# Attention and gated MLP on one core: features dealt to partitions in runs of five instead of chunks of 128

## The chip, the cores and the metric

The kernel runs on one core of one Trainium2 chip. The metric is the device time of one execution in microseconds (us); the time of a kernel is the median of several runs.

## What is computed

One block over 2048 tokens of 640 features (bf16): a LayerNorm without gain or bias, then windowed attention (32 heads of 20, window of 8 positions that are 2 apart) and a bilinear gated MLP (1536 wide) side by side. The reference, cut to what matters:

```python
xn = (x - mean(x)) / sqrt(var(x) + 1e-5)
q, k, v = split(xn @ wqkv)                      # 640 -> 3 x 640
logits[s, w] = q[s] . k[s - 2 * w] / sqrt(20)   # w = 0..7, masked before the start
o = (softmax(logits) * v[s - 2 * w]).sum(w) @ wo
h = (xn @ w_gate) * (xn @ w_up)                 # 640 -> 1536
out = x + o + h @ w_down
```

## The kernel before, in words

A token's features must lie on partitions to be contracted by TensorE (PE): a matmul sums over the 128 partitions of its two operands, and the 640 features make five such sums (NCH = 5 "chunks"), accumulated in PSUM. Every weight with the features as rows is therefore held as [128 partitions, 5 chunks, columns]: `WQKV` (three groups of 640 columns), `WG` and `WU` (1536 columns). The normalised activations are held in `XNT` as [128 partitions, 5 chunks, 2048 tokens]. For a sum over features it doesn't matter which feature lies on which partition and chunk, as long as the weights and XNT agree. Before, feature 128c + p lies on partition p of chunk c.

The tokens come in 16 tiles of 128. A tile of x is loaded with tokens on partitions into `XST` (14 slots), so its 640 features are one row. VectorE (DVE) takes the statistics in two halves (`ln_stats_a`, `ln_stats_b`, lines 372 and 378), merges them (`ln_aggr`, line 384); ScalarE takes the square root (line 385), DVE the reciprocal (`ln_rstd`, line 404). `ln_apply` (line 419) writes (x - mean) * rstd into `XNS`, a ring of four slots, with a tensor_scalar instruction. Tile 1 has its sums from ScalarE (`ln_sums`). Then the tile is turned:

- tiles 0 to 3 (NTP = 4) by PE, chunk by chunk (`ln_pe`, line 434), into PSUM, and from there into XNT by DVE or ScalarE (`ln_copy`, lines 445 and 447). For tile 0, `ln_apply` writes chunk 0 first and the other four after it; for tile 1, two chunks and then three.
- tiles 4 to 15 by a DMA transpose that the SP queue issues (line 423), straight from XNS into XNT. SP issues its DMAs in program order: behind the transpose of tile 7 stand the loads of x for tiles 13 to 15, behind that of tile 15 `late_loads`, the mask, WG and WU.

The first stage of PE is laid out by hand (lines 713 to 780). It warms up, transposes tile 0, projects queries for it (`proj_tile`, line 492) and tile 1, then keys of both tiles in a loop over chunks (line 773), in the middle of which, ahead of chunk 2's second and chunk 3's first matmul, the transposes of tiles 2 and 3 stand. After that come queries and keys of tiles 2 and 3 (`proj_wide`, line 499), and then blocks of 512 tokens (`proj`, line 475): values of the first block (25 matmuls), queries and keys of the second (tiles 4 to 7), the third and the fourth, then the other values. `ln_pace` puts LayerNorm's steps for the later tiles between these in program order, by a modelled time of 1.45 us a tile; since each engine has its own queue, that fixes only the order on ScalarE and DVE.

The weights of queries and keys come as ten loads of one chunk each (`wqkv_load`, SP queue), those of values as one. The weight columns are read by PE with a step of five (`wcols`), so that output feature 5i + m of a projection lands on partition i of group m; this step is along the columns and is in both versions.

Behind LayerNorm DVE multiplies queries with shifted keys (line 522), adds, and sums over a head's partitions by DMAs (lines 533 and 545); softmax follows (lines 551 to 582, the exponential on ScalarE), then the products with values (line 605). PE meanwhile runs the MLP: gate and up (`glu`, line 638), evacuated by ScalarE (line 640) and multiplied by DVE (line 643), and the down projection together with `wo` (lines 665 and 697). The order of all this comes from a list of work for PE (`fill`) that is dealt out between DVE's steps by modelled durations (`step`, `run_fill`, lines 852 to 874). PSUM's eight banks go round in a ring.

Of the kernel before, what the change touches and what calls it, by code (L numbers as in the profile page):

```python
# [11 lines left out]
NCH = 5  # L12
# [199 lines left out]
def build_kernel(nc, A_x, A_wqkv, A_wo, B_x, B_w_gate, B_w_up, B_w_down, out):  # L212
# [80 lines left out]
    def dma(o, i, r=(), w=(), name="", eng="sp", group=None):  # L293
        return op(eng, lambda e: e.dma_start(o, i), r=r, w=w, dma=True, name=name, group=group)  # L294
# [15 lines left out]
    def x_load(t, eng="sp"):  # L310
        dma(XST[:, t % NXS, :], xhbm[t * TS:(t + 1) * TS, :], w=[XST[:, t % NXS, :]], name=f"xld{t}", eng=eng)

    def x_load2(t):
        dst = XST[:, t % NXS:t % NXS + 2, :]
        dma(dst, xhbm[t * TS:(t + 2) * TS, :].rearrange("(u p) n -> p u n", p=TS), w=[dst], name=f"xld{t}")

    wqkv_src = A_wqkv.rearrange("(c p) n -> p c n", p=128)

    def wqkv_load(g, c=None, eng="sp"):
        cs = slice(0, NCH) if c is None else c  # L320
# [23 lines left out]
    def late_loads():  # L344
        dma(MASK[0:128:4], MSK0[0:32], r=[MSK0[0:32]], w=[MASK[0:128:4]], name="mask")
        for T, src in ((WG, B_w_gate), (WU, B_w_up)):
            dma(T[:], src.rearrange("(c p) n -> p c n", p=128), w=[T[:]], name="ld_w")

    def down_loads():
        dma(WD[:], B_w_down.rearrange("(c p) n -> p c n", p=128), w=[WD[:]], name="ld_wd")  # L350
# [49 lines left out]
    def ln_rstd(t):  # L400
        if t >= NT:
            return
        sd, rstd = SD[:, t, 0:1], SD[:, t, 1:2]
        op("dve", lambda e: e.reciprocal(rstd, sd), r=[("sd", t)], w=[("rstd", t)], name=f"rstd{t}")

    def ln_apply(t, between=None):
        if t >= NT:
            return
        x, xs, mv = XST[:, t % NXS, :], XNS[:, t % NXN, :], MV[:, t, 0:2]
        sd, rstd = SD[:, t, 0:1], SD[:, t, 1:2]  # L410
        op0 = ALU.add if t == 1 else ALU.subtract
        mean = ("nm", t) if t == 1 else mv
        if between is None:
            ln_rstd(t)
        else:
            between()
        for c0, c1 in {0: ((0, 128), (128, D)), 1: ((0, 256), (256, D))}.get(t, ((0, D),)):
            o, i = xs[:, c0:c1], x[:, c0:c1]
            op("dve", (lambda o, i: lambda e: e.tensor_scalar(o, i, mv[:, 0:1], rstd, op0=op0, op1=ALU.mult))(o, i),
               r=[i, mean, ("rstd", t)], w=[o], name=f"lnap{t}")  # L420
        if t >= NTP:
            o = XNT[:, :, t * TS:(t + 1) * TS]
            op("sp", lambda e: e.dma_start_transpose(o, xs), r=[xs], w=[o], dma=True, name=f"xT{t}")
        if t == 7:
            x_load(13)
            x_load2(14)
        if t == NT - 1:
            late_loads()
# [35 lines left out]
    def wcols(which, c, m):  # L464
        return WQKV[:, which, c, m:D:NCH]
# [252 lines left out]
    ln_sums(1, 1)  # L718
    ln_sums(1, 2)
    ln_apply(0)  # L720
    ln_pe(0)
    ln_copy(0, (0, 1, 2))
    ln_apply(1)
    warm(2, TS)

    def ln_next(t):
        ln_stats_b(t)
        ln_aggr(t)
        ln_stats_a(t + 1)
        ln_apply(t)  # L730
# [35 lines left out]
    for c in range(NCH):  # L766
        for m in range(NCH):
            if (c, m) in ((2, 1), (3, 0)):
                tr(c)
            o = PS[:, bm, 2 * TS:] if m == 4 else PS[:, 3 + m // 2, m % 2 * 2 * TS:(m % 2 + 1) * 2 * TS]  # L770
            l, x = wcols(1, c, m), XNT[:, c, 0:2 * TS]
# [182 lines left out]
def bass_parallel_sum__sliding_local_dilated__glu_gated_bilinear__prompt_kernel(  # L954
    nc, A_x, A_wqkv, A_wo, B_x, B_w_gate, B_w_up, B_w_down, out
):
    build_kernel(nc, A_x, A_wqkv, A_wo, B_x, B_w_gate, B_w_up, B_w_down, out)
# [28 lines left out]
```

## Time and profile before

| what | us |
|---|---|
| median of 7 runs | 252.62 |
| lowest and highest | 252.32, 253.22 |
| the profiled execution | 252.96 |
| its span, first to last instruction | 251.7 |
| PE busy | 247.4 |
| DVE busy | 215.9 |
| ScalarE (ACT) busy | 114.7 |
| GpSimd (POOL) busy | 32.6 |

PE, PEld, DVE, ACT and POOL are the engines, PEld being PE's weight loads; SPq is the SP queue. A line of groups gives the line of the code, the engine, the operation, what it writes and reads with its shape, how often it ran, then the busy time in us, the mean of one in ns, and the idle time of the engine just before it with what ended it. A line of the timeline gives the start in us, the duration in us, engine, line and operation; in brackets stands how long the engine was idle before and what it waited for. Where several instructions are merged (x2), the duration runs from the start of the first to the end of the last.

### The profile page before, as it was taken

Reading aid. Unit: us, or ns where it says so; the run is one execution under the profiler, and the core shown is the slowest. Engines: PE = TensorE matmul, PEld = TensorE weight load, DVE = VectorE, ACT = ScalarE, POOL = GpSimd, SP = SyncE. Lnnn points to the kernel's source line nnn. Section 1 sums busy time; section 2 is a strip of 40 time slices with the busy share of each in tenths; the row PEclk is TensorE's granted clock in tenths of the full one; section 3 lists DMA queues with packets and bytes.
Section 4 is the critical chain, followed back from the end, with each engine's and each line's share of the span. In section 5 each row is a group of like instructions: output and inputs, shape, how many; then the busy total and the mean of one; then the engine's idle time right before and its main releaser. Section 6 shows DMA issues by size and latency. Waiting matters only on the chain.

```text
span 251.7 us, 3246 instructions
## 1 busy us (share of the span) xinstructions
PE 247.4 (98%) x1274; PEld 129.0 (51%) x1294; DVE 215.9 (86%) x255; ACT 114.7 (46%) x203; POOL 32.6 (13%) x41
## 2 busy tenths in 40 slices
PE   8999999999999999999999999999999999999997
PEld 3895555555544444444444444444444444445775
DVE  4799699999999962999999994799999999997212
ACT  5486667555555557555555551315555111011000
POOL 1000001043345222002231101002000000200200
DMA  6999869854787473255369972197600011490561
GB/s 186 298 284 168 126 141 411 223 111 79 146 146 135 72 137 54 113 224 97 70 121 254 393 230 42 33 334 61 96 0 3 21 26 36 59 131 21 79 154 52
DMA packets 33775, 33.78 MB, mean 134 GB/s; under 512 B 17984, under 2 KB 30272, under 8 KB 33728
## 3 DMA queue, kind: packets, MB, share of 16 engines
q1 hardware_dynamic: 27280, 24.13, 34.4%
q0 software_dynamic: 6192, 9.31, 22.9%
q8 instruction: 10, 0.16, 0.3%
q10 hardware_dynamic: 288, 0.13, 0.2%
q14 instruction: 5, 0.04, 0.1%
HBM read 14.42 MB, written 4.59 MB: 76 GB/s over the span
## 4 chain that ended last, share of the span: by engine, by line
PE 95%; DMA 2%; SPq 2%; issue 1%; DVE 0%
PE PS L638 41%; PE PS L665 22%; PE PS L475 21%; PE PS L697 7%; PE PS L499 2%; DMA WQKV<-in_A_wqkv_dram 2%; SPq L294 2%; PE PS L773 1%; PE PS L434 0%; DVE FOUT L701 0%
## 5 line engine op out<-in xcount | busy, mean ns | idle before, releaser
L638 PE MATMUL PS<-XNT,WU 128*128 128x512 bf16 x237 | 59.0, 379 | 0.2
L638 PE MATMUL PS<-XNT,WG 128*128 128x512 bf16 x232 | 57.9, 379 | 0.4
L475 PE MATMUL PS<-XNT,WQKV 128*128 128x512 bf16 x245 | 53.7, 379 | 0.3
L605 DVE TENSOR_TENSOR PVB<-VO,ATB 128x10240 f16<-128x10240 bf16 x8 | 43.9, 5489 | 0.2
L475 PEld LDWEIGHTS PS<-XNT,WQKV 128*128 128x128 bf16 x250 | 29.4, 118 | 24.4
L640 ACT ACTIVATE USX<-PS 128x512 bf16<-128x512 f32 x48 | 28.7, 597 | 22.6 <-PE PS L638 22.6
L638 PEld LDWEIGHTS PS<-XNT,WU 128*128 128x128 bf16 x240 | 23.5, 98 | 28.3
L638 PEld LDWEIGHTS PS<-XNT,WG 128*128 128x128 bf16 x240 | 23.5, 98 | 28.3
L600 DVE TENSOR_TENSOR PVB<-PVB 128x5120 f16<-128x5120 f16 (+1 forms) x16 | 34.5, 2154 | 0.3
L533 POOL DMA_DIRECT2D LOG<-PE x24 | 21.6, 912 | 60.6 <-DMA LOG<-PE 60.6
L640 ACT ACTIVATE HT<-PS 128x512 bf16<-128x512 f32 x36 | 21.5, 597 | 16.4 <-PE PS L638 16.4
L671 ACT ACTIVATE DT<-PS 128x512 f16<-128x512 f32 x15 | 8.9, 596 | 42.3 <-PE PS L665 39.2
L665 PE MATMUL PS<-HT,WD 128*128 128x512 bf16 x118 | 27.4, 379 | 0.1
L522 DVE TENSOR_TENSOR TMP<-QH,KH 128x2048 f16<-128x2048 bf16 x16 | 19.1, 1216 | 0.0
L665 PEld LDWEIGHTS PS<-HT,WD 128*128 128x128 bf16 x120 | 11.7, 98 | 14.2
L522 DVE TENSOR_TENSOR PP<-QH,KH 128x2048 f16<-128x2048 bf16 x16 | 18.9, 1217 | 0.0
L527 DVE TENSOR_TENSOR PP<-PP,TMP 128x4096 f16<-128x4096 f16 x8 | 18.3, 2291 | 0.2
L665 PE MATMUL PS<-VO,WO 128*128 128x512 bf16 x74 | 18.4, 379 | 0.0
L701 DVE TENSOR_TENSOR FOUT<-PS,XR 128x320 bf16<-128x320 f32 (+2 forms) x9 | 4.1, 454 | 15.0 <-PE PS L697 15.0
L533 POOL DMA_DIRECT2D PE<-PP x8 | 8.4, 1045 | 61.6 <-DVE PP L528 61.6
L482 ACT ACTIVATE VO<-PS 128x512 bf16<-128x512 f32 x20 | 11.9, 597 | 8.9 <-PE PS L475 8.8
L643 DVE TENSOR_TENSOR HT<-HT,USX 128x512 bf16<-128x512 bf16 x36 | 14.3, 415 | 1.7 <-ACT USX L640 1.7
(71 smaller groups left out, 221.4 us busy)
## 6 DMA issues: line engine op xcount, KB each, us to landing
PE<-PP POOLq DMA_DIRECT2D x8, 512.0 KB, 5.0
ATB<-LOG SPq DMA_DIRECT2D x8, 512.0 KB, 4.8
LOG<-PE POOLq DMA_DIRECT2D x24, 128.0 KB, 2.7
WG<-in_B_w_gate_dram SPq DMA_DIRECT2D x1, 1920.0 KB, 8.1
WU<-in_B_w_up_dram SPq DMA_DIRECT2D x1, 1920.0 KB, 14.7
WD<-in_B_w_down_dram SPq DMA_DIRECT2D x1, 1920.0 KB, 11.6
out_dram<-in_A_x_dram SPq DMA_DIRECT2D x1, 1920.0 KB, 10.6
out_dram<-FACC POOLq DMA_DIRECT2D x3, 640.0 KB, 6.7
```

Source lines behind the costliest of these rows:

```text
L475: op("pe", (lambda l, x, c: lambda e: e.matmul(PS[:, b, :], l, x, start=(c == 0), stop=(c == NCH - 1)))(l, x, c), r=[l, x], w=[PS[:, b, :] ...
L482: op("act", lambda e: e.activation(o, PS[:, b, :], ACT.Copy, scale=sc), r=[PS[:, b, :]], w=[o], name=f"pev{which}_{m}_{j}")
L522: return (1.22, lambda: op("dve", lambda e: e.tensor_tensor(o, qw, kw, ALU.mult), r=[q, k], w=[o], name=f"prod{h}_{p}_{c}"))
L527: (2.3, lambda: op("dve", lambda e: e.tensor_tensor(a, a, b, ALU.add), r=[a, b], w=[a], name=f"psum{h}_{p}")),
L533: op("pool", lambda e: e.dma_start(o, i, accum_op=ALU.add), r=[o, i], w=[o], dma=True, name=name)
L600: return lambda: op("dve", lambda e: e.tensor_tensor(o, x, y, ALU.add), r=[x, y], w=[o], name=f"{name}_{b}")
L605: lambda: op("dve", lambda e: e.tensor_tensor(PVB[:], vw, aw, ALU.mult), r=[v, a], w=[PVB[:]], name=f"pv_{b}")),
L638: op("pe", (lambda l, x, c: lambda e: e.matmul(PS[:, b, :], l, x, start=(c == 0), stop=(c == NCH - 1)))(l, x, c), r=[l, x], w=[PS[:, b, :] ...
L640: op("act", lambda e: e.activation(o, PS[:, b, :], ACT.Copy), r=[PS[:, b, :]], w=[o], name=f"guev{which}_{m}_{j}")
L643: h_pending.append(lambda: op("dve", lambda e: e.tensor_tensor(h, h, o, ALU.mult), r=[h, o], w=[h], name=f"h{m}_{j}"))
L665: op("pe", (lambda l, x, i: lambda e: e.matmul(PS[:, b, :], l, x, start=(i == 0), stop=(i == n - 1)))(l, x, i), r=[l, x], w=[PS[:, b, :]], ...
L697: op("pe", (lambda l, x, i, b, wid: lambda e: e.matmul(PS[:, b, 0:wid], l, x, start=(i == 0), stop=(i == n - 1)))(l, x, i, b, wid), r=[l, ...
```

## The change

Feature 5p + c now lies on partition p of chunk c, for the weights that are contracted over the features of the normalised activations: `WQKV`, `WG` and `WU`. The weights' rows are taken as "(p c)" instead of "(c p)". LayerNorm's write puts the features into the row of XNS in the new order (chunk by chunk, and within a chunk features c, 5 + c, 10 + c and so on), so its source is read with a step of five elements; the destination is the same row as before. Everything behind XNS is as it was: the transposes, XNT's shape, the matmuls and their number, and what comes out of them but for the order of summation. `WD` and `WO` are not touched.

```diff
-    wqkv_src = A_wqkv.rearrange("(c p) n -> p c n", p=128)
+    wqkv_src = A_wqkv.rearrange("(p c) n -> p c n", p=128)
...
         for T, src in ((WG, B_w_gate), (WU, B_w_up)):
-            dma(T[:], src.rearrange("(c p) n -> p c n", p=128), w=[T[:]], name="ld_w")
+            dma(T[:], src.rearrange("(p c) n -> p c n", p=128), w=[T[:]], name="ld_w")
...
         for c0, c1 in {0: ((0, 128), (128, D)), 1: ((0, 256), (256, D))}.get(t, ((0, D),)):
-            o, i = xs[:, c0:c1], x[:, c0:c1]
+            o = xs[:, c0:c1].rearrange("q (c p) -> q c p", p=128)
+            i = x.rearrange("q (p c) -> q c p", c=NCH)[:, c0 // 128:c1 // 128]
             op("dve", (lambda o, i: lambda e: e.tensor_scalar(o, i, mv[:, 0:1], rstd, op0=op0, op1=ALU.mult))(o, i),
                r=[i, mean, ("rstd", t)], w=[o], name=f"lnap{t}")
```

## The prediction, as put on record before the change was run

> **What bounds the kernel now.** I read the page's busy times first, then the chain that ended last, then the timeline of the first 40 us (the only stretch whose instructions the change touches), and last the idle times of VectorE (DVE) further on.
>
> ```profile
> PE 247.4 (98%) x1274; PEld 129.0 (51%) x1294; DVE 215.9 (86%) x255; ACT 114.7 (46%) x203; POOL 32.6 (13%) x41
> PE 95%; DMA 2%; SPq 2%; issue 1%; DVE 0%
> ```
>
> TensorE (PE) is busy from end to end and makes up 95% of the chain. Behind the start there is no gap in it: whatever delays PE in the first 25 us comes out at the end in full, and whatever delays only DVE costs nothing until PE waits for it. Now the start, from the timeline:
>
> ```profile
> 9.95 0.40 DVE L419 TENSOR_SCALAR XNS<-XST,MV,SD 128x640 bf16<-128x640 bf16 x1
> 10.60 0.45 DVE L419 TENSOR_SCALAR XNS<-XST,MV,SD 128x640 bf16<-128x640 bf16 x1
> 10.84 0.30 PE L773 MATMUL PS<-XNT,WQKV 128*128 128x256 bf16 x1 [0.28 <-DMA WQKV<-in_A_wqkv_dram]
> 11.69 0.44 PE L434 MATMUL PS<-IDENT,XNS 128*128 128x128 bf16 x5
> 12.11 0.49 DVE L372 BATCH_NORM_STATS2 STATS<-XST 128x6 f32<-128x320 bf16 x1 [0.40 <-DMA XST<-in_A_x_dram]
> 14.57 6.30 SPq L423 DMA_TRANSPOSE XNT<-XNS  x4
> 18.44 0.39 DVE L419 TENSOR_SCALAR XNS<-XST,MV,SD 128x640 bf16<-128x640 bf16 x1
> 18.74 21.53 PE L475 MATMUL PS<-XNT,WQKV 128*128 128x512 bf16 x98
> ```
>
> The first two lines normalise tiles 2 and 3; the second ends at 11.05, and PE transposes that tile from 11.59 (weight load) or 11.69. So there is half a microsecond between them. At 10.84 PE waits for a WQKV chunk, the last wait on the chain. DVE waits 0.40 us for x at 12.11. Tile 7 is normalised by 18.83 and its DMA transpose is issued at 19.58, since SP is busy with the earlier ones (1.28 us each); it lands 3.6 us later, at 23.2. PE wants tiles 4 to 7 after 25 matmuls of 216 ns from 18.74, at 24.13: 0.93 us of slack.
>
> The operation that the change rewrites, and two weight loads that differ in their step:
>
> ```profile
> L419 DVE TENSOR_SCALAR XNS<-XST,MV,SD 128x640 bf16<-128x640 bf16 x14 | 5.7, 410 | 1.9 <-DMA XNT<-XNS 1.9
> L475 PEld LDWEIGHTS PS<-XNT,WQKV 128*128 128x128 bf16 x250 | 29.4, 118 | 24.4
> L638 PEld LDWEIGHTS PS<-XNT,WU 128*128 128x128 bf16 x240 | 23.5, 98 | 28.3
> ```
>
> And where a late DVE is made good:
>
> ```profile
> 90.58 0.42 DVE L643 TENSOR_TENSOR HT<-HT,USX 128x512 bf16<-128x512 bf16 x1 [1.71 <-ACT USX L640]
> 96.92 1.90 ACT L572 ACTIVATE LOG<-LOG 128x2048 f16<-128x2048 f16 x1
> 98.85 0.69 DVE L553 TENSOR_TENSOR S<-LOG 128x1024 f16<-128x1024 f16 x1 [4.95 <-ACT LOG L572]
> ```
>
> DVE idles 1.71 us, then hands its logits over at 93.95; the exponential stands in ScalarE's queue behind other work and starts 3.0 us after that. A DVE that is up to 4.7 us late against PE loses it all here.
>
> [...] 128 elements took 313 ns, 640 took 410[...]. [...] No DVE row of the kernel before reads with a step of 5. [...]
>
> **The change, part by part.**
>
> *WQKV loads.* Each of the ten chunk loads still takes 128 pieces of 1,280 bytes, the value load 640 of them; only the distance between rows grows. Same count, same bytes, same SP issue (432 ns each). I take 0. Bounds: PE waits for these loads 0.28 us at 10.84 and its weight loads 0.19 at 7.49, so an earlier landing gains 0.47 at most; 10% on the 4.87 us of the gating load would cost 0.5.
>
> *Gate and up weights.* A partition's five rows become one run of 15,360 bytes instead of five of 3,072. They are issued at 34.37 and 34.99 and landed by 49.7; PE first needs them at 72.7. Faster or slower, 23 us cover it. Cost 0. They move later by what the last transpose is late (about 5 us below), which the same 23 us cover.
>
> *LayerNorm's write (line 419), 18 instructions.* They now read bf16 with a step of 10 bytes[...]. The destination stays one contiguous run. [...] For the step itself I take the nearest row: weight loads with the same step of five take 118 against 98 ns, a factor of 1.2 (an estimate[...]). [...] **+0.63 us each, 1.04 instead of 0.41**. [...] The pieces of tiles 0 and 1 with 1, 4 and 2 chunks[...]: +0.05, +0.19, +0.09; the one with 3 chunks[...]: +0.38.
>
> Now the path, with +0.63:
> - Tile 0: +0.24 on DVE, of which a 0.17 wait for ScalarE's square root (6.24) hides all but 0.07. Tile 1: +0.07 +0.47, ends 7.62 instead of 7.08. PE's matmuls behind its transposes move from 7.50 to about 7.85; the wait for WQKV at 10.84 takes 0.28 of that, 0.07 is left.
> - Tile 2's statistics start 0.09 later (the copies before them end at 8.0 against x at 7.91). Tile 2 ends 10.35 + 0.09 + 0.63 = 11.07: PE's transposes are 0.27 late. Tile 3 ends 11.05 + 0.09 + 2 x 0.63 = 12.40, transposes at 12.45 instead of 11.59: **PE +0.86**. This contains the earlier delays.
> - The PSUM copy that follows on DVE (0.36) ends at 12.76, so tile 4's statistics start 0.65 late, the 0.40 wait for x gone. Tile 7 ends 18.83 + 0.65 + 4 x 0.63 = 22.0; SP is free by then and issues at 22.1; landing 2.7 to 3.6 later, 3.2 taken: 25.3. PE asks at 24.13 + 0.86 = 25.0: **PE +0.3**.
> - Tiles 8 to 15 go at 1.36 + 0.63 = 2.0 us each, 8 us for four, where PE spends 10.8 on four: no more waits. The two waits of DVE for a free XNS slot (1.9 us) vanish.
> - DVE ends LayerNorm near 37.3 instead of 30.9, but its first products waited for queries and keys until 35.5 anyway, so it is some 6 us late, 5 against PE. The gap around 90 to 98 takes 4.7, the rest is a wait of 0.3 on ScalarE, under PSUM's eight banks of 1.08 us each. Cost 0; without that cover it would be up to 5 us.
>
> Sum: 0.86 + 0.3 = **1.2 us**. The profiled execution took 252.96 (span 251.7 and 1.26 around it), so 254.2 for it; it is 0.34 over the median of the runs, so the median goes from 252.62 to **253.8**.
>
> **Rivals.**
> *[...] (not slower).* +0.23 each. Tile 3 ends at 11.05 + 0.46 = 11.51 before PE's 11.59, and the copy after it at 11.9, before x at 12.11. Tile 7 ends at 19.75, issued at 19.85 and landed by 23.5, before 24.13. All hidden: 252.6 to 252.7. It decides for every increment under about 0.25[...].
> *Every element pays a jump.* +0.94. Tile 3 ends near 13.3, PE +1.8; tile 4 starts 1.6 late, tile 7 ends 18.83 + 1.6 + 3.8 = 24.2, lands 27.5, PE asks at 25.9: another 1.6. Total 3.4: 256.0. DVE is then 7 us late against PE, 2.6 beyond the gap, which PSUM's banks and 2.4 us ahead of the down projection (152.77) nearly cover. [...]
> *The WQKV loads change.* Earlier landings with a cheap write: 252.1 to 252.3; later ones, 0.5 more than the forecast.
>
> **How the numbers follow.** Forecast (increments of 0.5 to 0.75): 0.46, 253.1 to 254.6. [...] Jump at every element: 0.24, of it 0.06 beyond 256.2. Loads faster 0.05, slower 0.05. 0.2% is 0.5 us, about what a measurement of this kernel can tell from no change. Faster: the fast loads, 0.05. Same: [...]little of the forecast's lower end, 0.23. Slower: 0.72. The range 252.3 to 256.2 leaves out the fast loads' half, the far tail of the jump and the slow loads on top of it.
>
> **What would show it.** Line 419's mean for 640 elements: 0.64[...], 0.9 to 1.05 (forecast), 1.35 or more (jump). PE idle before L434 near 12 us with DVE named, and before L475 near 25 us with the transposes named. DVE's waits for XNS gone, its 4.95 us at 98.85 shrunk. WG and WU landing unchanged in length. I am wrong if PE's start shows longer waits on WQKV, or if a wait on DVE appears behind 100 us.

## The result, and the profile after

The changed kernel takes 253.49 us (median of 14 runs, 253.22 to 253.99) against 252.67 us (35 runs of the kernel before, 252.25 to 253.31): a ratio of 1.0031, 95% interval 1.0024 to 1.0038, or some 0.8 us more. The forecast was 253.8, in a range of 252.3 to 256.2.

The profiled execution took 253.48 us, just the median, with a span of 252.2. That of the kernel before (252.96) had been 0.29 above its median, so the two traces show only 0.5 of the 0.8 us; more on the other 0.3 comes below, under the WQKV loads.

From the page of the changed kernel, busy times and the chain by engine (code lines from 419 on have moved down by one):

```profile
PE 247.3 (98%) x1274; PEld 128.7 (51%) x1294; DVE 223.5 (89%) x255; ACT 113.5 (45%) x203; POOL 32.5 (13%) x41
PE 94%; DVE 2%; DMA 2%; SPq 1%; issue 1%
```

PE has the same work. DVE has 7.6 us more, and it now appears in the chain, with 2%. Where, the timeline of the start tells:

```profile
10.10 0.94 DVE L420 TENSOR_SCALAR XNS<-XST,MV,SD 128x640 bf16<-128x640 bf16 x1
11.10 0.45 PE L435 MATMUL PS<-IDENT,XNS 128*128 128x128 bf16 x5 [0.33 <-DVE XNS L420]
11.15 1.01 DVE L420 TENSOR_SCALAR XNS<-XST,MV,SD 128x640 bf16<-128x640 bf16 x1
12.21 0.45 PE L435 MATMUL PS<-IDENT,XNS 128*128 128x128 bf16 x5 [0.22 <-DVE XNS L420]
12.34 0.48 DVE L372 BATCH_NORM_STATS2 STATS<-XST 128x6 f32<-128x320 bf16 x1
15.35 6.94 SPq L424 DMA_TRANSPOSE XNT<-XNS  x4
20.11 0.95 DVE L420 TENSOR_SCALAR XNS<-XST,MV,SD 128x640 bf16<-128x640 bf16 x1
19.27 21.10 PE L476 MATMUL PS<-XNT,WQKV 128*128 128x512 bf16 x96
```

The profile now names DVE's write as what PE's transposes of tiles 2 and 3 wait for, and the wait for WQKV at 10.84 is gone. The long run of 512-wide matmuls starts at 19.27 instead of 18.74, and nothing is added behind it: tile 7 is written by 21.06, its transpose is issued at 21.1 and landed 2.6 us later, at 23.7; PE asks 25 matmuls after 19.27, at 24.67. The chain that ended last, from its pieces in order of time (start, duration, what), shows what decides PE's start now:

```profile
4.02 4.01 DMA XST<-in_A_x_dram
10.18 0.86 DVE XNS L420
11.15 1.02 DVE XNS L420
12.21 0.45 PE PS L435 x5
```

Before, it was a load of WQKV, on which PE itself waited. Now it is the load of tile 2's x, DVE's statistics and its two writes, and then PE's transposes of tile 3.

The write itself, by shape, from the groups of the changed kernel:

```profile
L420 DVE TENSOR_SCALAR XNS<-XST,MV,SD 128x640 bf16<-128x640 bf16 x14 | 13.5, 967 | 0.1
L420 DVE TENSOR_SCALAR XNS<-XST,MV,SD 128x384 bf16<-128x384 bf16 x1 | 0.7, 716 | 0.0
L420 DVE TENSOR_SCALAR XNS<-XST,MV,SD 128x512 bf16<-128x512 bf16 x1 | 0.6, 553 | 0.0
L420 DVE TENSOR_SCALAR XNS<-XST,MV,SD 128x256 bf16<-128x256 bf16 x1 | 0.4, 422 | 0.0
L420 DVE TENSOR_SCALAR XNS<-XST,MV,SD 128x128 bf16<-128x128 bf16 x1 | 0.3, 349 | 0.0
```

Two rates stand here. Odd numbers of chunks (5 and 3): (967 - 716) / 256 = 0.98 ns an element. Even ones and the single chunk (4, 2, 1): (553 - 349) / 384 = 0.53 ns, half of it; 512 elements take less time than 384. The waits of DVE for a free XNS slot are gone too (0.1 in all, from 1.9).

Further on, DVE's first addition (line 528) behind the products starts at 41.31 instead of 36.8, 4.5 us late, or 4.0 late against PE, which is itself 0.5 late. The gap around 90 to 98 us swallows it:

```profile
97.44 1.90 ACT L573 ACTIVATE LOG<-LOG 128x2048 f16<-128x2048 f16 x1
99.38 0.69 DVE L554 TENSOR_TENSOR S<-LOG 128x1024 f16<-128x1024 f16 x1 [2.76 <-ACT LOG L573]
```

The 1.71 us of idle before it are used up, the 4.95 have become 2.76 (3.9 used in all), and DVE resumes 0.53 us later than before, just as late as PE. The logits were handed over at 96.62, 0.8 us before the exponential: that is what was left.

### The profile page after: what moved, and what is told of

Same layout as the page of the kernel before. It is cut to its first block, busy times and chain, and to the rows that moved or that the text cites. A ratio compares the mean times of both kernels' runs of the same rounds, so it can differ in the third digit from the quotient of the medians.

```text
span 252.2 us, 3246 instructions
## 1 busy us (share of the span) xinstructions
PE 247.3 (98%) x1274; PEld 128.7 (51%) x1294; DVE 223.5 (89%) x255; ACT 113.5 (45%) x203; POOL 32.5 (13%) x41
## 4 chain that ended last, share of the span: by engine, by line
PE 94%; DVE 2%; DMA 2%; SPq 1%; issue 1%
PE PS L639 41%; PE PS L666 22%; PE PS L476 21%; PE PS L698 7%; PE PS L500 2%; DMA XST<-in_A_x_dram 2%; SPq L294 1%; DVE XNS L420 1%; PE PS L774 0%; DVE STATS L372 0%; DVE STATS L378 0%; PE PS L435 0%; DVE MV L384 0%; DVE FOUT L702 0%; DVE SD L404 0%
## 5 line engine op out<-in xcount | busy, mean ns | idle before, releaser
L534 POOL DMA_DIRECT2D PE<-PP x8 | 7.6, 954 | 65.6 <-DVE PP L529 65.6
L420 DVE TENSOR_SCALAR XNS<-XST,MV,SD 128x640 bf16<-128x640 bf16 (+4 forms) x18 | 15.4, 866 | 0.1
```

The source lines that it names most:

```text
L534: op("pool", lambda e: e.dma_start(o, i, accum_op=ALU.add), r=[o, i], w=[o], dma=True, name=name)
```

## The experiments

Theory A: the cost is the write of tiles 2 and 3, which PE's transposes wait for; everything else is hidden. Theory B: the loads with their new row pitch (19,200 bytes instead of 3,840) cost (or save) time. Theory C: every tile's write costs, through the DMA transposes or through a late DVE.

**One half of the change alone.** First the weights' order without LayerNorm's:

```diff
-            o = xs[:, c0:c1].rearrange("q (c p) -> q c p", p=128)
-            i = x.rearrange("q (p c) -> q c p", c=NCH)[:, c0 // 128:c1 // 128]
+            o, i = xs[:, c0:c1], x[:, c0:c1]
```

> Only the loads of the changed kernel: WQKV, WG and WU are taken in the new order, LayerNorm writes its columns as before with a contiguous source. The features of weights and activations then don't match, so the sums are other ones; the instructions and their sizes are those of the kernel before. Theory A (the cost is the slower write of tiles 2 and 3, which PE's transposes wait for): no slower than before, 252.4 to 252.8; if the new row pitch brings WQKV in earlier, as the landing of 3.8 instead of 4.9 us for the gating chunk suggests, the wait for WQKV at 10.84 is gone and up to 0.3 us are gained. Theory B (the loads with the new pitch cost something themselves): 0.3 us or more slower than before. Theory C (every tile's write costs): as A.

Measured: 252.72 us, ratio to the kernel before 1.0007 (0.9998 to 1.0015). Then LayerNorm's order with the old one of the weights ("(c p)" again in both loads):

> Only the write of the changed kernel: LayerNorm's columns in the new order, all weights loaded in the old one, so the features don't match and the sums are other ones. Theory A and C: as slow as the changed kernel, 253.3 to 253.8, with the write at 0.97 us for 640 elements. Theory B: nearer to the time before, below 253.1. If WQKV's landing is later than in the changed kernel, that comes from the pitch; then some tenths may be added, up to 0.3.

Measured: 253.24 us, ratio 1.0021 (1.0011 to 1.0031), with the write at 966 ns. So the write carries the cost and the loads none that can be measured (by the interval, 0.4 us at most); theory B falls, in both directions. The new pitch brings nothing in earlier either. The chunk that gated PE at 10.84 lands, counted from its issue, after 4.9 us in the profile before, but after 3.9 with the old pitch here and 4.2 with the new one in the run ahead: the late landing belongs to that one execution, not to the pitch. It cost more than the 0.28 us that PE idled, since PE's weight loads waited 0.53: from the first matmul of the keys to the long run the profile before has 9.47 us, where the three profiles below in which PE has no wait have 8.96. It is likely that this put the profile before 0.3 us above its median; no second profile of that kernel shows it.

**Early tiles against late ones.** The step for tiles 0 to 3 alone:

```diff
             i = x.rearrange("q (p c) -> q c p", c=NCH)[:, c0 // 128:c1 // 128]
+            if t >= NTP:
+                o, i = xs, x
```

> The changed kernel, but tiles 4 to 15 are written with a contiguous source (their features then don't match the weights'); only tiles 0 to 3 are read with the step of five. Theory A: the time of the changed kernel, 253.3 to 253.7, with DVE ending LayerNorm near 31 us again instead of 35.5. Theory C (late tiles cost too, through the DMA transposes or a late DVE): back by more than half, to 253.0 or less.

Measured: 253.42 us, ratio 1.0031 (1.0021 to 1.0041), the same as the whole change. DVE's last LayerNorm write starts at 30.30, much as before the change (30.54). Then the other way round: tiles 2 and 3 freed of the slow write, with the step moved to PE:

```diff
             i = x.rearrange("q (p c) -> q c p", c=NCH)[:, c0 // 128:c1 // 128]
+            if t in (2, 3):
+                o, i = xs, x
...
-            i = XNS[:, t % NXN, c * 128:(c + 1) * 128]
+            i = XNS[:, t % NXN, c:D:NCH] if t in (2, 3) else XNS[:, t % NXN, c * 128:(c + 1) * 128]
```

> The changed kernel, but tiles 2 and 3 are written with a contiguous source, and PE's transposes of these two tiles take every fifth column of them instead; tiles 0, 1 and 4 to 15 are as in the changed kernel. The features match again. Theory A: the wait of PE for the two writes near 11 and 12 us is gone, 252.4 to 252.9, the weight loads of these ten transposes at about 118 instead of 98 ns. Theory B: as slow as the changed kernel. Theory C (every tile counts alike): two of sixteen tiles, so 253.4.

Measured: 252.63 us, ratio 1.0001 (0.9993 to 1.0009): the loss is gone, though twelve late tiles still pay 0.97 us each. From its timeline, PE's two transposes and the long run:

```profile
10.43 0.44 PE L437 MATMUL PS<-IDENT,XNS 128*128 128x128 bf16 x5
11.15 0.44 PE L437 MATMUL PS<-IDENT,XNS 128*128 128x128 bf16 x5
18.19 2.10 PE L478 MATMUL PS<-XNT,WQKV 128*128 128x512 bf16 x9
```

Neither waits for DVE. The mean of the 20 transposes' weight loads is 108 ns, which is what ten at 118 and ten at 98 make. With these four runs theory C falls as well, for the change as it is, and the cost is that of the writes of tiles 2 and 3.

**A shorter write for tiles 2 and 3.** Two ways. In one, their destination gets a pitch of 144 elements per chunk, so that it stays five rows like the source:

```diff
+    XNP = sb("XNP", [128, 2, NCH, 144], at=a_us + 2304)
...
+            if t in (2, 3):
+                o = XNP[:, t - 2, :, 0:128]
...
+            i = XNP[:, t - 2, c, 0:128] if t in (2, 3) else XNS[:, t % NXN, c * 128:(c + 1) * 128]
```

If five rows at the destination help, such a write was to take 0.69 us, and else the 0.97 of the changed kernel:

> The changed kernel, but tiles 2 and 3 are written into a buffer whose chunks lie 144 elements apart, so source and destination are both five rows and neither is one run; PE's transposes read it from there. [...] 0.69 us instead of 0.97; tile 2 is 0.28 and tile 3 0.56 us earlier, and by theory A the time falls by about 0.5, to 252.8 to 253.1. [...] 0.97 us, 253.3 to 253.6. By theory B (loads) or C (all tiles): 253.3 or more in both cases.

Measured: 252.76 us, ratio 1.0012 (1.0006 to 1.0019). Its groups:

```profile
L423 DVE TENSOR_SCALAR XNS<-XST,MV,SD 128x640 bf16<-128x640 bf16 x12 | 11.6, 965 | 0.0
L423 DVE TENSOR_SCALAR XNP<-XST,MV,SD 128x640 bf16<-128x640 bf16 x2 | 1.4, 692 | 0.0
```

Same source, same number of elements, 692 instead of 965 ns once the destination has five rows too: 0.27 of the 0.56 us by which a write has grown hang on the one run of 640 at the destination. At the faster of the two rates above, 640 elements would take 0.62 us (an estimate: 349 ns for the first 128, 0.53 for each of the other 512). In the other way each write is cut into four chunks and one:

```diff
-        for c0, c1 in {0: ((0, 128), (128, D)), 1: ((0, 256), (256, D))}.get(t, ((0, D),)):
+        for c0, c1 in {0: ((0, 128), (128, D)), 1: ((0, 256), (256, D)), 2: ((0, 512), (512, D)),
+                       3: ((0, 512), (512, D))}.get(t, ((0, D),)):
```

> The changed kernel, but the writes of tiles 2 and 3 are cut in two instructions, four chunks and one[...], as tile 0 has them: 0.55 and 0.35 us, together 0.82 from start to end in tile 0's case, instead of 0.97. Tile 2 is ready 0.14 and tile 3 0.28 us earlier; by theory A the time falls by 0.2 to 0.3, to 253.1 to 253.3, about half of what the padded buffer gains. Theories B and C: 253.4 to 253.5.

Measured: 252.73 us, ratio 1.0007 (0.9999 to 1.0015). The direction is as expected, the size a miss: more was gained than 0.2 to 0.3, as much as by the padding (the two intervals overlap). The trace shows three parts. The two instructions overlap, so that the next one starts 0.70 and 0.75 us after tile 2's and tile 3's first (0.86 and 0.92 in the changed kernel), which gives 0.33 at tile 3. The second part was missing from the expectation: PE need not wait for the second piece, in which only the last chunk lies. Here are that piece of tile 3, and the weight loads of PE's transposes of this tile:

```profile
11.02 0.35 DVE L421 TENSOR_SCALAR XNS<-XST,MV,SD 128x128 bf16<-128x128 bf16 x1
11.15 0.37 PEld L436 LDWEIGHTS PS<-IDENT,XNS 128*128 128x128 bf16 x5
```

The first four chunks are written by 11.07 (from 10.52, in 0.55 us), the loads begin at 11.15, and the second piece ends only at 11.37. The third part is luck of this profile: tile 2's x landed 3.3 us after its issue, against 4.0 in the profile of the changed kernel, and so tile 2's write starts at 9.63 against 10.10. How the gain of the median divides among these isn't settled.

**How far the cover reaches.** Writes made twice, of tiles 4 to 7 in one run, of 8 to 15 in the other:

```diff
-        for c0, c1 in {0: ((0, 128), (128, D)), 1: ((0, 256), (256, D))}.get(t, ((0, D),)):
+        cuts = {0: ((0, 128), (128, D)), 1: ((0, 256), (256, D))}.get(t, ((0, D),))
+        for c0, c1 in cuts * (2 if 4 <= t < 8 else 1):
```

> The changed kernel, but LayerNorm's write of tiles 4 to 7 is made twice (the same bytes, 0.96 us more of VectorE for each). Theory A says that these writes cost nothing only since they are covered: tile 7's transpose lands near 23.7 and PE asks at 24.67, 1 us of cover. With 4 x 0.96 = 3.8 us more, tile 7 ends near 24.9 and lands at 27.6 to 28.5: PE waits 2.9 to 3.9 us ahead of the projections of the second block, 256.4 to 257.5. A theory by which late tiles are free whatever they cost: 253.5.

Measured: 258.42 us, ratio 1.0245 (1.0223 to 1.0266). That is 0.9 us above the expected range. Where PE waits, and its granted clock around it (columns of the windows: stretch, its length, busy time with number of instructions of PE, PEld, DVE, ACT and POOL, clock, DMA share, GB/s):

```profile
27.46 14.83 PE L477 MATMUL PS<-XNT,WQKV 128*128 128x512 bf16 x59 [3.29 <-DMA XNT<-XNS]
24.00:28.00 4.00, 0.71 (x4) 0.35 (x4) 4.00 (x11) 1.21 (x5) 0.00 (x0) 1.00 0.35 80
28.00:29.00 1.00, 1.00 (x5) 0.42 (x4) 1.00 (x3) 0.51 (x2) 0.00 (x0) 0.61 1.00 332
29.00:31.00 2.00, 2.00 (x6) 0.66 (x5) 2.00 (x6) 1.26 (x3) 0.00 (x0) 0.50 0.89 165
31.00:32.00 1.00, 1.00 (x5) 0.44 (x4) 1.00 (x4) 0.46 (x2) 0.00 (x0) 0.68 0.30 60
32.00:36.00 4.00, 3.95 (x19) 2.22 (x19) 4.00 (x11) 1.72 (x5) 0.00 (x0) 1.00 0.60 72
```

The wait for tile 7 is there at the size expected, 3.29 us, ended by the DMA transpose. Another 1.8 us are PE's own: soon after the wait its clock is granted at half for some 3.4 us (an estimate from the windows: 0.39, 1.00 and 0.32 us lost, at 0.50), and the first 25 matmuls take 7.28 us where 49 at full clock take 10.74 (5.48 for 25). The two make 5.1 us; with a long run that starts 0.44 us earlier than in the changed kernel they account for the 4.7 us between the two profiled executions.

> The changed kernel, but the write of tiles 8 to 15 is made twice (0.96 us more each, 7.7 in all). The transposes of tiles 11 and 15 then still land about when PE asks for them (35.3 against 35.5, 45.9 against 46.3), so PE's start doesn't move; VectorE enters attention 7.7 us later. Theory A with the prediction's cover of about 4.7 us, of which the changed kernel has used most: ScalarE stands still ahead of the exponential, PSUM's ring is used up or nearly, and the values' products come late for the first down projection, 256 to 258.5. If a late VectorE is simply free: 253.5.

Measured: 258.35 us, ratio 1.0233 (1.0219 to 1.0247). The time is in the range expected. From the waits of this run, and from the chain that ended last:

```profile
ACT SD L385 <- DVE MV L384: 17.2, 12, 2.2
ACT LOG L574 <- DVE LOG L572: 6.2, 2, 4.1
PE PS L477 <- ACT QH L484: 2.2, 2, 1.7
PE PS L667 <- DVE VO L602: 1.7, 1, 1.7
157.23 0.83 DVE VO L602
158.10 6.22 PE PS L667 x28
```

ScalarE does stand still ahead of the exponential, up to 4.1 us, and the down projection waits 1.7 us for the values' products, until 158.10. From there the chain goes back through DVE (with ScalarE between, at the exponential) to the start of LayerNorm: DVE's lateness decides the end, by the path that was expected. What the expectation didn't have is that PE waits earlier, too (2.2 us for evacuated queries and another 0.4 for keys, at 34 to 40 us): LayerNorm's square roots stand in ScalarE's queue among the evacuations, each waits for DVE's statistics, and behind it PSUM isn't emptied. These waits lie beside the chain; without them PE would have stood longer at 158.10. In the changed kernel the same waits of ScalarE add up to 11.4 us (5.0 before), and PE shows no wait on them. So theory A keeps its second half: late writes are covered, and not free.

## Why the prediction was right

By its own steps:

- *What bounds.* Right: PE's start decides, and its delay comes out at the end in full. In the eight kernels that change no more than the start, the time of the profiled execution less the start of the first 512-wide matmul is the same, 234.20 to 234.25 us:

| kernel | first matmul of the keys | first 512-wide matmul | profiled execution |
|---|---|---|---|
| step on PE | 9.23 | 18.19 | 252.42 |
| weights alone | 9.32 | 18.28 | 252.53 |
| split | 9.34 | 18.30 | 252.50 |
| padded | 9.53 | 18.60 | 252.84 |
| before | 9.27 | 18.74 | 252.96 |
| late plain | 9.40 | 19.03 | 253.26 |
| write alone | 9.38 | 19.10 | 253.35 |
| whole change | 9.40 | 19.27 | 253.48 |

  In the first three PE goes through from the keys to the long run in 8.96 us. In the last three the long run comes 11.2 us after DVE's first statistics of tile 2 (at 7.83, 7.88 and 8.06): there DVE's chain sets the start, and PE loses 0.7 to 0.9 us to it.
- *Loads of WQKV, gate and up: 0.* Right. PE's waits on WQKV didn't grow: 0.28 us, at 7.03, where the profile before has 0.28 and 0.19. WG landed after 7.7 us in pieces of 15,360 bytes, and after 7.7 in pieces of 3,072 when it was issued as late (write alone).
- *The write: 0.41 to 1.04 us.* Right in kind: 640 elements take 0.97, within the 0.9 to 1.05 of the forecast, and the write grew by 0.56 us instead of 0.63. The pieces with 1, 4 and 2 chunks grew by 0.04, 0.15 and 0.07 (from 313, 404 and 349 ns), where 0.05, 0.19 and 0.09 were forecast, the one with 3 by 0.34 (from 375) instead of 0.38. Why the two rates differ, the traces don't show. The time of an element behind the 0.63 was the author's estimate, which no trace shows, and so were the rivals' 0.23 and 0.94. The first comes near the write into five rows, 692 ns (0.28 more than the 410 before), which the change doesn't have; by the second the write would have taken 1.35 us.
- *The step of five: a factor of 1.2.* Not shown. It was taken from weight loads of PE, 118 against 98 ns, and that it holds for DVE was an estimate. In the traces of DVE the step comes together with the five rows: from 384 to 640 elements the kernel before took 0.14 ns an element ((410 - 375) / 256), the changed one 0.98. No run reads five rows without a step into one run, so the share of the step in the 0.56 us is open.
- *PE +0.86 at tile 3.* The mechanism was right. In the traces the long run moves by 0.53. The transposes' weight loads start at 12.21, not at the 12.45 of the prediction: each write grew by 0.07 less, and the gap between the two writes shrank from 0.25 to 0.11, since the square root for tile 3 was done while the longer write of tile 2 ran. Besides, the profile before had lost time to the late WQKV chunk, which the later wait for DVE covers; against the profiles without a wait PE loses 0.9 us.
- *From the profile to the median: less 0.34.* Wrong. The changed kernel's profile is at its median, so there was nothing to take off. In terms of the profile the forecast was 254.2 against 253.48. This error and the 0.33 too many at tile 3 have opposite signs and cancel in the median: that 253.8 is off by no more than tile 7's 0.3 is luck.
- *PE +0.3 at tile 7.* Wrong. The tile was written by 21.06 instead of 22.0, mostly because tile 4's statistics started at 12.34 and not at 12.76 and each write grew by less. The transpose then landed 2.6 us after its issue instead of 3.2: at 23.7 instead of 25.3, 1.0 us before PE asked. The late tiles alone would have had to be about 0.25 us slower each to show (an estimate: four writes to 1.0 us).
- *DVE's lateness: 0.* Right, by the gap that was named: DVE was 4.0 us late against PE, and 0.8 of the 4.7 are left. The prediction missed that ScalarE's square roots wait in the evacuations' queue; the cover was large enough for that here, and not with tiles 8 to 15 written twice.

1.2 us forecast, 0.8 measured: the term that did not come is tile 7's, and the wait at tile 3 is the whole.

## What to carry to other kernels

A reorder that "only" changes an access pattern can make an engine's instruction more than twice as long (here 967 ns instead of 410), and how much depends on both patterns: 3 and 5 rows into one run took 0.98 ns an element, 1, 2 and 4 rows 0.53, and 640 elements took 692 ns from five rows into five rows with gaps. Price such a change only where another engine stands waiting: here fourteen full writes grew by the same 0.56 us, and two of them made the whole difference. One profile is one execution, too: the one before held some 0.5 us of a late load, which the change then covered, and the two traces differ by 0.3 us less than the medians. And a cover is a number: LayerNorm's late tiles were free with 1.0 us to spare, and cost some 5 us when four or eight of them had grown by another 0.96 each.

## What the runs showed that was not expected

An idle stretch of PE of 3.29 us was followed by some 3.4 us at half the granted clock, which made the wait half as dear again (1.8 us). That the idle stretch is the cause is an inference from the order of time: all four executions of that kernel have a mean clock below 1.00 (0.987 to 0.993), and no execution of the other kernels has, not even with waits of PE of up to 1.7 us.
